# Threshold attention with a leaky-ReLU network: q of the first pair of heads is loaded and split in two pieces

## The chip, the cores and the metric

The kernel runs on one NeuronCore of a Trainium2 chip. A core has a matrix engine (TensorE, PE in the profile, with its weight loads as PEld), VectorE (DVE), ScalarE (ACT), GpSimd (POOL), and SyncE (SP), which in this kernel only issues DMAs. Each engine runs its own instructions in order and waits on semaphores for the others. Matrix results land in PSUM, all other tiles in SBUF. The metric is the device time of one execution in microseconds; the median of several runs is compared.

## The reference

Inputs are q, k, v of shape 8 x 8 x 576 x 64 (batch, heads, sequence, head size) in float32, a number tau = 0.02, and two weight matrices of 512 x 2048 and 2048 x 512.

```
scores = q @ k^T / 8
thresh = max(scores, last axis) - tau
scores = where(scores >= thresh, scores, -1e9)
attn   = exp(scores - max(scores))
attn   = attn / (sum(attn) + 1e-9)
x      = (attn @ v), heads joined to 4608 x 512
h      = x @ w_in
out    = max(0.01 * h, h) @ w_out          (4608 x 512, float32)
```

## The kernel before

The heads are taken two at a time. A *pair* p is two neighbouring heads of one batch; there are 32 pairs, and two pairs make a *chunk* c of nine *steps* t, each step one block of 128 rows of scores (the ninth holds the last 64 rows of both pairs). So the main loop (lines 406 to 480) runs 16 chunks of nine steps and one more chunk that finishes. All is emitted under a manual schedule (line 379): the order of instructions on each engine is the order of the program text.

**Loading.** `load_qk(p, i, tail)` (line 73) issues one DMA on SP's queue: for i = 0 q, for i = 1 k; without `tail` the first 512 rows as four tiles of 128 rows for both heads (256 KB, line 81), with `tail` the last 64 rows (32 KB, line 86). Both fill the tile `nat`, of which three buffers exist. Pair 0 is loaded first, in the order q, k, tail of q, tail of k (line 381). Then the identity matrix and some constants are made, and pairs 1 and 2 are loaded on the same queue (lines 395 to 398). Later pairs are loaded in the loop, two steps' worth ahead (lines 477 to 480); a load into a buffer waits until the pair that was there has been transposed.

**Splitting.** `prep(p, i)` (line 122) turns one operand of a pair round: PE transposes its tiles of 128 rows in float32 into PSUM (line 129; four tiles for q, five for k, since both tails travel with k), ScalarE scales and rounds them to the fp16 tile `hi` (line 138), and VectorE computes the remainder `lo` in fp16 (line 139). The remainder is not emitted at once but put on the list `soon`, which is run at the end of the step (line 467; for pair 0 right behind the two calls, line 401). The PSUM tile of `prep` is A, with a single buffer of two banks; only the k of pair 0 uses a buffer of the scores' tile s instead (line 400). A is also used by the value matmuls and sums of later chunks. A new user of A waits for the last reader of the one before.

**A step.** `s_mm(c, t)` (line 145, matmuls at line 158) computes the scores of one block for both heads as three products, hi hi + lo hi + hi lo, into two s tiles, of which two buffers exist. `s_max` (line 167) runs once per head: VectorE copies the scores out with a sign and takes the row maximum (tile sn, line 181), GpSimd adds tau (nth, line 186), and ScalarE takes the exponential, either plainly (tile e, line 191) or with the threshold in it (tile far, line 197, then W, line 201, with a read of the accumulated row sum). `s_mask` (line 206) applies the threshold on VectorE for the plain ones, one step later, and sends W through a transposing DMA on SP's queue (line 220). In steps 0 and 1 of chunk 0 `prep` of pair 1 stands between the score matmuls and the maxima (lines 429 to 431): q in step 0, k in step 1.

**The rest.** From the second chunk on the values are multiplied (line 279), and from the third on units of the two dense layers (matmuls at lines 301 and 316) are dealt out over the steps by fixed shares. Weights and v come in over GpSimd's queue from step 1 on.

The order of the start is, on PE: transposes of pair 0's q, of its k, scores of step 0, transposes of pair 1's q, scores of step 1, transposes of pair 1's k, scores of step 2.

Of the kernel before, what the change touches and what calls it, by code (L numbers as in the profile page):

```python
# [10 lines left out]
FP16 = mybir.dt.float16  # L11
OP = mybir.AluOpType
AF = mybir.ActivationFunctionType
# [3 lines left out]
def kernel(  # L17
# [10 lines left out]
    nc = tc.nc  # L28
# [8 lines left out]
    QS = 64.0  # L37
# [4 lines left out]
    sb = ctx.enter_context(tc.tile_pool(name="sb", bufs=1))  # L42
# [18 lines left out]
    nat, qk, wTs, xTs = {}, {}, {}, {}  # L61
# [5 lines left out]
    def pair_of_banks(tag="A", bufs=1):  # L67
        return ps.tile([128, 2, 512], FP32, tag=tag, bufs=bufs, name=tag)
# [1 line left out]
    def bank():  # L70
        return ps.tile([128, 512], FP32, tag="u", bufs=2, name="u")

    def load_qk(p, i, tail):

        b, g = divmod(p, NG)
        if p not in nat:
            nat[p] = sb.tile([128, 9, 2, 64], FP32, tag="nat", bufs=3, name="nat")
        t = nat[p]
        h2 = (q, k)[i][b, 2 * g:2 * g + 2, :, :]
        if not tail:  # L80
            nc.sync.dma_start(
                out=t[0:128, 4 * i:4 * i + 4, :, :],
                in_=h2[:, 0:512, :].rearrange("h (p c) d -> p c h d", c=4),
            )
        else:
            nc.sync.dma_start(
                out=t[ds(64 - 64 * i, 64), 8, :, :],
                in_=h2[:, 512:576, :].rearrange("h p d -> p h d"),
            )
# [23 lines left out]
    def take(fs):  # L113
        r = list(fs)
        fs.clear()
        return r

    def run(fs):
        for f in fs:
            f()  # L120

    def prep(p, i, tag="A", bufs=1):


        t = nat[p]
        pt = pair_of_banks(tag, bufs).rearrange("p a b -> p (a b)")
        for c in range(4 + i):

            nc.tensor.matmul(  # L129
                out=pt[0:128, ds(c * 128, 128)],  # L130
                lhsT=t[0:128, 4 * i + c, :, :].rearrange("p h d -> p (h d)"),
                rhs=I32[:, :],
                is_transpose=True, skip_group_check=True,
            )
        N = 512 + 128 * i
        hi = sb.tile([128, N], FP16, tag=f"hi{i}", bufs=3, name=f"hi{i}")
        lo = sb.tile([128, N], FP16, tag=f"lo{i}", bufs=3, name=f"lo{i}")
        nc.scalar.activation(out=hi[:, :], in_=pt[:, 0:N], func=AF.Copy, bias=0.0, scale=QS)  # L138
        soon.append(lambda: nc.vector.scalar_tensor_tensor(  # L139
            out=lo[:, :], in0=pt[:, 0:N], scalar=QS, in1=hi[:, :],  # L140
            op0=OP.mult, op1=OP.subtract,
        ))
        qk.setdefault(p, {})[i] = (hi, lo)

    def s_mm(c, t):

# [75 lines left out]
    inv, rows, rcs = {}, {}, {}  # L222
# [9 lines left out]
    def sums_1(c):  # L232
        d1, rr = inv[c]
        nc.vector.reciprocal(out=rr[:, :], in_=d1[:, :])
        nc.gpsimd.tensor_scalar(out=r2[:, 0, 0:18], in0=rr[:, :], scalar1=1.0 / RS, scalar2=0.0,
                                op0=OP.mult, op1=OP.add)
# [58 lines left out]

    def h_unit(N, xs, g_out, j0, nj):

        t = bank()
        for j in range(nj):
            for gi in range(NG):  # L300
                nc.tensor.matmul(  # L301
                    out=t[:, ts(j, N)], lhsT=w_in16[:, gi, ts(j0 + j, 128)], rhs=xs[gi],
                    start=(gi == 0), stop=(gi == NG - 1), skip_group_check=True,
                )
        nc.scalar.activation(out=g_out, in_=t[:, 0:nj * N].rearrange("p (j n) -> p j n", j=nj),  # L305
                             func=AF.Prelu, bias=0.0, scale=1.0, alpha=0.01)
# [68 lines left out]
    def work(n):  # L375
        for _ in range(min(n, len(units))):
            units.pop(0)[1]()

    with tc.manual_schedule():
        nc.scalar.preload_act_table_set("natural_log_exp_and_others")  # L380
        for i, tail in ((0, 0), (1, 0), (0, 1), (1, 1)):
            load_qk(0, i, tail)
        make_identity(nc, I32)
        nc.vector.tensor_copy(out=I16[:, :], in_=I32[:, :])
        nc.vector.memset(ntau[:, :], -tau_f)
        nc.vector.memset(r2[:, :, :], 0.0)
        nc.vector.tensor_tensor(
            out=sel[:, :, :], in0=I32[:, 0:18].unsqueeze(2).to_broadcast([128, 18, 64]),
            in1=I32[:, 64:82].unsqueeze(2).to_broadcast([128, 18, 64]), op=OP.add,
        )  # L390
        nc.vector.tensor_scalar(out=sel[:, :, :], in0=sel[:, :, :], scalar1=RS, scalar2=None, op0=OP.mult)
        for t in Vs:
            nc.vector.memset(t[64:128, :, 0, 4, :], 0.0)
            nc.vector.memset(t[0:64, :, 1, 0, :], 0.0)
        for p in range(1, 3):
            for i in range(2):
                for tail in range(2):
                    load_qk(p, i, tail)
        prep(0, 0)
        prep(0, 1, "s", 2)  # L400
        run(take(soon))
        share = (23, 27, 23, 13, 23, 13, 23, 23, 23)
        credit = 0.0
        w_at = [1 + i for i in range(32)]
        prev = None
        for c in range(NC + 1):
            last = c == NC
            for t in range(NT):
                step = c * NT + t
                if c > 1 and c % 2 == 0 and t == 6:  # L410

                    if c % 4 == 2 and c > 2:
                        push_tail(c // 2 - 3, 1)
                    push_main(c // 2 - 1)
                    if c % 4 == 0:
                        push_tail(c // 2 - 2, 0)
                    if last:
                        push_tail(c // 2 - 2, 1)
                if not last:
                    s_mm(c, t)  # L420


                nxt = {6: (2 * c + 2, 0), 7: (2 * c + 2, 1), 8: (2 * c + 3, 0), 0: (2 * c + 1, 1)}
                if c == 0:
                    nxt[0], nxt[1] = (1, 0), (1, 1)
                pi = nxt.get(t)
                if pi is not None and pi[0] >= NP:
                    pi = None
                if c == 0 and t < 2:
                    prep(*pi)  # L430
                    pi = None

                if c > 0 and t in (3, 5):
                    values(c - 1, t // 2 - 1)

                ahead = [share[i % NT] for i in range(step, (c // 2 * 2 + (0 if c % 2 == 0 and t < 6 else 2)) * NT + 6)]
                credit = min(credit, 1.0) + (len(units) - credit) * share[t] / sum(ahead)
                n = min(int(credit + 0.01), len(units))
                credit -= n
                if not last:  # L440


                    direct = tau_f <= 16.0 and (
                        t not in (3, 7) if c < 3 else t in (3, 5) or not any(u[0] for u in units[:n]))
                    s_max(c, t, 0, False)
                if c > 0 and t == 1:
                    sums_1(c - 1)
                work(n - n // 2)
                if pi is not None:
                    prep(*pi)  # L450
                if c > 0 and t in (2, 4):
                    sums_4(c - 1, t // 2 - 1)
                if not last:
                    s_max(c, t, 1, direct)
                if c > 0 and t == 1:
                    sums_2(c - 1)
                    work(n // 2 - 1)
                    sums_3(c - 1)
                    work(1 if n > 1 else 0)
                else:  # L460
                    work(n // 2)
                if prev is not None:
                    s_mask(*prev)
                    prev = None
                if not last:
                    prev = (c, t)
                run(take(soon))
                if c > 0 and t == 0:
                    sums_0(c - 1)
                if c == 0 and 0 < t < 6:  # L470
                    load_v(0, t - 1)
                if c % 2 == 0 and c > 0 and t >= 4 and c // 2 < B:
                    load_v(c // 2, t - 4)
                for i in range(32):
                    if w_at[i] == step:
                        load_w(i)
                if t < 4 and 2 * c + 3 < NP:
                    load_qk(2 * c + 3, t // 2, t % 2)
                elif 4 <= t < 8 and 2 * c + 4 < NP:
                    load_qk(2 * c + 4, t // 2 - 2, t % 2)  # L480
        work(len(units))
# [35 lines left out]
```

## Time and profile before

| what | value |
| --- | --- |
| median of 3 runs | 540.57 us (540.03 to 540.68) |
| span of the profiled execution, first to last instruction | 538.3 us |
| mean granted TensorE clock over the span | 0.967 |
| PE busy | 497.8 us, 92% |
| ScalarE busy | 433.8 us, 81% |
| VectorE busy | 421.7 us, 78% |
| GpSimd busy | 188.1 us, 35% |
| first load issued, first transpose, first maximum | 0.75, 4.59, 10.13 us |

Of the profiled execution the span is given; it is 2.3 us shorter than the median of the timed runs, which also hold what lies before the first and after the last instruction. The profile gives, for each group of instructions, the count, the busy time and the mean of one; for each row of the timeline the start, the length, the engine, the line of the kernel, the operation and the tiles written and read, and in brackets how long the engine stood idle before and what released it. Rows that begin with SPq or ACTq are issues of DMAs by that engine's queue. In a table by windows each row has the window, its length, the busy time with the number of instructions in brackets, the granted clock, the DMA engines' share and the rate in GB/s.

### The profile page before, as it was taken

How to read it: one execution, taken by the hardware profiler on the slowest of the kernel's cores; microseconds unless marked ns; L12 is line 12 of the kernel's file. 1: busy time of each engine (PE TensorE's matmuls, PEld its weight loads, DVE VectorE, ACT ScalarE, POOL GpSimd, SP SyncE). 2: the span in 40 equal slices, each digit the busy share in tenths (PEclk: the TensorE clock that was granted, in tenths of full speed). 3: DMA queues.
4: the chain of work that ended last, by engine and by line, in shares of the span. 5: the costliest groups of instructions: out<-in, count | busy, mean ns of one | idle time of the engine just before them, and what ended most of it. 6: DMA issues, size and time to landing. Idle time of an engine off the chain costs nothing.

```text
span 538.3 us, 12333 instructions
## 1 busy us (share of the span) xinstructions
PE 497.8 (92%) x4384; PEld 272.8 (51%) x4384; DVE 421.7 (78%) x1106; ACT 433.8 (81%) x765; POOL 188.1 (35%) x430
## 2 busy tenths in 40 slices
PE   5678679899999999999999999999999999999996
PEld 3345454454545565454545566455545566445444
DVE  4897989988899878987899878987899878982000
ACT  3887879899878989889888989889888989884622
POOL 0754556443433334222432234323432234331000
PEclk9676969999999999999999999999999999999999
DMA  6999999998998699778999799777998699654001
GB/s 151 150 202 161 175 182 214 200 180 173 172 165 136 139 169 196 140 137 153 183 155 143 132 182 185 142 135 159 183 155 136 132 187 135 111 89 106 39 40 58
DMA packets 266814, 80.50 MB, mean 150 GB/s; under 512 B 251905, under 2 KB 264193, under 8 KB 266753
## 3 DMA queue, kind: packets, MB, share of 16 engines
q1 hardware_dynamic: 249136, 70.68, 72.3%
q0 software_dynamic: 17536, 8.92, 14.2%
q8 instruction: 34, 0.56, 0.4%
q14 instruction: 28, 0.22, 0.1%
q10 hardware_dynamic: 80, 0.13, 0.1%
HBM read 36.70 MB, written 9.44 MB: 86 GB/s over the span
## 4 chain that ended last, share of the span: by engine, by line
PE 43%; ACT 25%; DVE 16%; issue 8%; DMA 4%; POOL 3%; SPq 0%; DVEq 0%; ACTq 0%; POOLq 0%
PE u L316 13%; DVE sn L181 11%; PE u L301 10%; PE s L158 10%; PE A L279 8%; ACT e L191 7%; ACT far L197 5%; ACT W L201 5%; DVE W L214 3%; ACT gM L305 3%; ACT hi L138 3%; POOL nth L186 3%; DMA nat<-in_q_dram 2%; DVE lo L139 1%; ACT rc L268 1%
## 5 line engine op out<-in xcount | busy, mean ns | idle before, releaser
L181 DVE TENSOR_SCALAR_CACHE_REDUCE sn<-s 128x576 f32<-128x576 f32 x288 | 206.5, 750 | 49.3 <-PE s L158 49.1
L186 POOL TENSOR_SCALAR nth<-nmx 128x1 f32<-128x1 f32 x288 | 127.4, 442 | 251.7 <-DVE sn L181 229.5
L191 ACT ACTIVATE e<-sn,nmx 128x576 f16<-128x576 f32 x196 | 150.5, 769 | 32.4 <-DVE sn L181 32.2
L214 DVE SCALAR_TENSOR_TENSOR W<-sn,nth,e 128x576 f16<-128x576 f32 x196 | 155.6, 814 | 0.0
L301 PE MATMUL u<-xT,win 128*128 128x512 f16 x512 | 128.9, 380 | 2.5 <-ACT gM L305 2.5
L316 PE MATMUL u<-wout,gM 128*128 128x512 f16 x512 | 126.2, 380 | 0.0
L158 PEld LDWEIGHTS <-hi 64*128 64x128 f16 (+1 forms) x1280 | 65.1, 99 | 70.2 <-issue 54.9
L158 PE MATMUL s<-hi,hi 64*128 64x288 f16 x512 | 86.2, 300 | 10.3 <-DVE sn L181 8.8
L158 PE MATMUL s<-lo,hi 64*128 64x288 f16 (+1 forms) x640 | 92.2, 294 | 0.0
L158 PE MATMUL s<-hi,lo 64*128 64x288 f16 (+1 forms) x640 | 92.1, 294 | 0.0
L301 PEld LDWEIGHTS <-win 128*128 128x128 f16 x768 | 58.7, 98 | 56.5 <-issue 20.1
L305 ACT ACTIVATE gM<-u 128x512 f16<-128x512 f32 x128 | 74.6, 588 | 11.7 <-PE u L301 11.7
L197 ACT ACTIVATE far<-sn,nth 128x576 f32<-128x576 f32 x92 | 71.0, 771 | 13.8 <-POOL nth L186 11.6
L201 ACT ACTIVATE W<-far,ntau 128x576 f16<-128x576 f32 x92 | 71.3, 775 | 3.0
L316 PEld LDWEIGHTS <-gM 128*128 128x128 f16 x512 | 44.7, 98 | 51.3 <-issue 12.3
L139 DVE SCALAR_TENSOR_TENSOR lo<-A,hi 128x512 f16<-128x512 f32 (+1 forms) x63 | 47.6, 756 | 14.2 <-ACT hi L138 13.7
L129 PE MATMUL A<-I,nat 128*128 128x128 f32 x283 | 44.6, 288 | 9.9 <-DVE lo L139 4.7
L279 PE MATMUL A<-wT,V 128*64 128x288 f16 x640 | 47.5, 297 | 1.5 <-ACT rc L268 1.1
L129 PEld LDWEIGHTS A<-I,nat 128*128 128x128 f32 x283 | 35.2, 147 | 25.2 <-DVE lo L139 10.0
L138 ACT ACTIVATE hi<-A 128x512 f16<-128x512 f32 (+1 forms) x63 | 40.0, 636 | 7.6 <-PE A L129 7.6
L279 PEld LDWEIGHTS <-V 128*64 128x64 f16 x640 | 36.6, 113 | 11.9 <-issue 8.4
L158 PEld LDWEIGHTS <-lo 64*128 64x128 f16 (+1 forms) x640 | 32.1, 99 | 12.6 <-issue 8.9
(44 smaller groups left out, 292.1 us busy)
## 6 DMA issues: line engine op xcount, KB each, us to landing
nat<-in_q_dram SPq DMA_DIRECT2D x32, 256.0 KB, 3.8
nat<-in_k_dram SPq DMA_DIRECT2D x32, 256.0 KB, 3.9
out_dram<-osb SPq DMA_DIRECT2D x16, 512.0 KB, 3.0
wT<-W SPq DMA_TRANSPOSE x144, 3.9
V<-in_v_dram POOLq DMA_DIRECT2D x8, 256.0 KB, 6.1
win<-in_moe_w_in_dram POOLq DMA_DIRECT2D x16, 128.0 KB, 5.2
V<-in_v_dram POOLq DMA_DIRECT2D x16, 128.0 KB, 4.7
wout<-in_moe_w_out_dram POOLq DMA_DIRECT2D x16, 128.0 KB, 4.3
```

The source lines that it names most:

```text
L129: nc.tensor.matmul(out=pt[0:128, ds(c * 128, 128)], lhsT=t[0:128, 4 * i + c, :, :].rearrange("p h d -> p (h d)"), rhs=I32[:, :], is_transp ...
L158: nc.tensor.matmul(out=out[h][po, half, 0:288], lhsT=qk[p][i][a][r, cols], rhs=qk[p][1][b][r, ds(half * 288, 288)], start=(ti == 0), stop= ...
L181: nc.vector.tensor_scalar(out=sn[:, h, :].rearrange("p (a b) -> p a b", a=2), in0=s_[:, :, 0:288], scalar1=-BS, scalar2=None, op0=OP.mult, ...
L186: nc.gpsimd.tensor_scalar(out=nth[:, h:h + 1], in0=nmx[:, h:h + 1], scalar1=1.0, scalar2=tau_f, op0=OP.mult, op1=OP.add,)
L191: nc.scalar.activation(out=e[:, h, :], in_=sn[:, h, :], func=AF.Exp, bias=nmx[:, h:h + 1], scale=-1.0,)
L197: nc.scalar.activation(out=far[:, :], in_=sn[:, h, :], func=AF.Prelu, bias=nth[:, h:h + 1], scale=-1.0, alpha=BIG,)
L201: nc.scalar.activation(out=w[:, ds(h * 576, 576)], in_=far[:, :], func=AF.Exp, bias=ntau[:, 0:1], scale=1.0, accum_out=dens[c][:, 2 * t + ...
L214: nc.vector.scalar_tensor_tensor(out=w[:, ds(h * 576, 576)], in0=sn[:, h, :], scalar=nth[:, h:h + 1], in1=e[:, h, :], op0=OP.is_le, op1=OP ...
L279: nc.tensor.matmul(out=t[ds(h * 64, 64), half, 0:288], lhsT=vb[:, g, h, kb, :], rhs=wT[:, 4 * h + kb, ds(e * 576 + half * 288, 288)], star ...
L301: nc.tensor.matmul(out=t[:, ts(j, N)], lhsT=w_in16[:, gi, ts(j0 + j, 128)], rhs=xs[gi], start=(gi == 0), stop=(gi == NG - 1), skip_group_c ...
L305: nc.scalar.activation(out=g_out, in_=t[:, 0:nj * N].rearrange("p (j n) -> p j n", j=nj), func=AF.Prelu, bias=0.0, scale=1.0, alpha=0.01)
L316: nc.tensor.matmul(out=t[:, :], lhsT=g_in(j), rhs=w_out16[:, j, :], start=(j == 0), stop=(j == NJ - 1), skip_group_check=True,)
```

## The change

`load_qk` can load a range of q's four tiles and can issue on another engine's queue. `prep` can split a range of tiles; the range's results go into columns of one shared pair of tiles hi and lo. With these, the start is arranged anew:

- On SP's queue: the first tile of pair 0's q (64 KB), then all of k, and then the other three tiles of q as two DMAs, one for each head (96 KB each).
- On ScalarE's queue, ahead of the load of its function table: the tails of q and k.
- Ahead of the loop only the first tile of q is split, then k with the tails.
- The other three tiles of q are split in step 0 of chunk 0, behind the scores of that step and ahead of the split of pair 1's q. Both splits use A, and both remainders are on `soon`, which runs at the end of the step.

```diff
-    def load_qk(p, i, tail):
+    def load_qk(p, i, tail, eng=nc.sync, c0=0, c1=4):
...
         if not tail:
-            nc.sync.dma_start(
-                out=t[0:128, 4 * i:4 * i + 4, :, :],
-                in_=h2[:, 0:512, :].rearrange("h (p c) d -> p c h d", c=4),
-            )
+            rows = h2[:, 0:512, :].rearrange("h (p c) d -> p c h d", c=4)[:, c0:c1, :, :]
+            for hs in (ds(0, 2),) if c1 - c0 in (1, 4) else (ds(0, 1), ds(1, 1)):
+                eng.dma_start(out=t[0:128, 4 * i + c0:4 * i + c1, hs, :], in_=rows[:, :, hs, :])
         else:
-            nc.sync.dma_start(
+            eng.dma_start(
...
-    def prep(p, i, tag="A", bufs=1):
+    def prep(p, i, tag="A", bufs=1, c0=0, c1=None):
...
+        c1 = c1 or 4 + i
         pt = pair_of_banks(tag, bufs).rearrange("p a b -> p (a b)")
-        for c in range(4 + i):
+        for c in range(c0, c1):
...
-        N = 512 + 128 * i
-        hi = sb.tile([128, N], FP16, tag=f"hi{i}", bufs=3, name=f"hi{i}")
-        lo = sb.tile([128, N], FP16, tag=f"lo{i}", bufs=3, name=f"lo{i}")
-        nc.scalar.activation(out=hi[:, :], in_=pt[:, 0:N], func=AF.Copy, bias=0.0, scale=QS)
+        if i not in qk.setdefault(p, {}):
+            qk[p][i] = [sb.tile([128, 512 + 128 * i], FP16, tag=f"{n}{i}", bufs=3, name=f"{n}{i}")
+                        for n in ("hi", "lo")]
+        w = ds(c0 * 128, (c1 - c0) * 128)
+        hi, lo = (x[:, w] for x in qk[p][i])
+        nc.scalar.activation(out=hi, in_=pt[:, w], func=AF.Copy, bias=0.0, scale=QS)
         soon.append(lambda: nc.vector.scalar_tensor_tensor(
-            out=lo[:, :], in0=pt[:, 0:N], scalar=QS, in1=hi[:, :],
-            op0=OP.mult, op1=OP.subtract,
-        ))
-        qk.setdefault(p, {})[i] = (hi, lo)
+            out=lo, in0=pt[:, w], scalar=QS, in1=hi, op0=OP.mult, op1=OP.subtract))
...
     with tc.manual_schedule():
+        load_qk(0, 0, 0, c1=1)
+        load_qk(0, 1, 0)
+        for i in range(2):
+            load_qk(0, i, 1, nc.scalar)
+        load_qk(0, 0, 0, c0=1)
         nc.scalar.preload_act_table_set("natural_log_exp_and_others")
-        for i, tail in ((0, 0), (1, 0), (0, 1), (1, 1)):
-            load_qk(0, i, tail)
...
-        prep(0, 0)
+        prep(0, 0, c1=1)
         prep(0, 1, "s", 2)
...
                 if c == 0 and t < 2:
+                    if t == 0:
+                        prep(0, 0, c0=1)
                     prep(*pi)
                     pi = None
```

## The prediction

> **What bounds the kernel now.** I read the page's busy shares first, then the chain of work that ended last, in order of time, and from it the timeline of the first 20 us, where the whole change lies.
>
> The page, shares of the span and granted clock in 40 slices of 13.5 us:
>
> ```profile
> PE 497.8 (92%) x4384; PEld 272.8 (51%) x4384; DVE 421.7 (78%) x1106; ACT 433.8 (81%) x765; POOL 188.1 (35%) x430
> ...
> PE   5678679899999999999999999999999999999996
> ...
> PEclk9676969999999999999999999999999999999999
> ```
>
> TensorE (PE) is the bound from slice 9 on; ahead of it no engine is full. What a start-up edit is worth must be read from the chain there (start, length, what):
>
> ```profile
> 0.75 0.78 SPq L81
> ...
> 1.58 4.10 DMA nat<-in_k_dram
> ...
> 5.73 1.34 PE s L129 x5
> ...
> 7.09 0.71 ACT hi L138
> ...
> 7.83 0.84 DVE lo L139
> ...
> 8.71 1.59 PE s L158 x11
> 10.30 1.05 PE A L129 x4
> 11.35 1.68 PE s L158 x11
> ...
> 13.05 0.25 DVE sn L181
> ```
>
> The reader is to see two things. The first scores wait for the landing of k at 5.68, not of q. And from there the chain hands over without a pause: transposes, split, scores of step 0, transposes of pair 1's q (the row at 10.30), scores of step 1. Later pieces of DMA in the chain are few (wT 3.28 us at 314, nat of q 6.83 at 322 and 4.32 at 388, out 2.27 at 333), and each is issued by SP behind the work of its own step, so it shifts along. A microsecond won or lost here moves everything behind it.
>
> The timeline around steps 0 to 2:
>
> ```profile
> 10.23 1.12 PE L129 MATMUL A<-I,nat 128*128 128x128 f32 x4
> ...
> 11.38 0.60 ACT L138 ACTIVATE hi<-A 128x512 f16<-128x512 f32 x1 [3.59 <-PE A L129]
> ...
> 12.01 0.69 DVE L139 SCALAR_TENSOR_TENSOR lo<-A,hi 128x512 f16<-128x512 f32 x1 [0.44 <-ACT hi L138]
> ...
> 15.25 0.82 DVE L139 SCALAR_TENSOR_TENSOR lo<-A,hi 128x640 f16<-128x640 f32 x1
> ...
> 15.99 0.75 DVE L181 TENSOR_SCALAR_CACHE_REDUCE sn<-s 128x576 f32<-128x576 f32 x1
> ```
>
> Today there is one user of PSUM tile A per step: four transposes, the ACT copy to hi, and the DVE remainder lo at the step's end. A has one buffer, so the next user of A waits for that lo.
>
> **The change, part by part.** The sum is made in differences on the profiled execution, whose span is 538.3 us. The runs' median is 540.57, so 2.3 us lie around the span; I add the same 2.3 after the change.
>
> *q's first load cut to a quarter, tails moved.* k is issued at 1.58 as today's second DMA, behind 64 KB in place of 256 KB. The loads of line 81 in the first 30 us show how soon one lands after its issue:
>
> ```profile
> DMA to landing us min/median/max: 3.6/3.8/7.3
> ```
>
> Today k took 4.10, so it was queued behind q for only 0.3 to 0.5 us. With the queue clear, k lands at 1.58 + 3.7 = 5.28: gain 0.4 us. Ends: a quarter-size q may also be issued in 0.62 instead of 0.78 and k then land after the fastest 3.55, gain 0.8; or the 64 KB of tails, sent at the same moment from the other queue, and two queues at once, delay it as far as today's later landings, loss 0.3 (k at 6.0). I take 0.4, by the median row.
>
> A rule of the Trainium skill speaks against the tails' new queue: in "DMA: Bandwidth & Descriptors", section "Issuing engines are not separate DMA queues", DMAs of SP and ScalarE run on the same 16 engines and interleave, and only issue time is saved. In the trace 3.0 to 4.5 us moved 240 to 290 GB/s, so 64 KB are about 0.22 us: by the rule the gain would be 0.2 instead of 0.4.
>
> *SP's queue.* Four issues before pair 1's (q, k, two tails: 0.75 to 3.90), four after (q tile 0, k, two halves of the other three tiles): the loads of pairs 1 and 2 keep their place within some tenths. Pair 1's q, issued at 3.90, lands 3.6 later, at 7.5, and is transposed at 10.2. The three q tiles, issued from about 2.3 and 3.0, land by about 7 and are wanted at 9.8. The load of pair 3's q, which waits at 9.5 for pair 0's last transposes, goes out some 1.2 us later; behind it on SP stands the transposing DMA of 15.3. All hidden.
>
> *ScalarE's queue.* Two issues go ahead of the table load (0.74, 1.28 long). SP's rows for the tails are 0.6 to 0.9 each, so the table is ready at 3.2 to 3.9 and not 2.0. ACT's first copy comes at 5.71 today; of q tile 0 it would be at about 4.2, and the one that counts, hi of k, at 6.7. Cost nothing; without k's wait it would cost 1.5. POOL's queue is not touched.
>
> *First split, q tile 0 alone.* One transpose instead of four; hi and lo of 128 columns, 0.3 each (512 to 640 columns cost 0.10 and 0.13 more, carried down). All before k lands. From k on everything is today's, so step 0's scores end 0.4 earlier: the moment E at which PE starts the transposes behind them moves from 10.23 to 9.83.
>
> *The three other tiles, in step 0.* This is the cost. Their transposes, hi and lo now stand between step 0's scores and pair 1's q, with both tile users on A's one buffer, and lo comes only after both of step 0's maxima on DVE. Counted from E:
> - three transposes: four need 1.15 to the ACT copy, five (13.15 to 14.52) 1.37; three 0.94. hi of 384 columns 0.48, to 1.42. DVE is free at 1.33 (second maximum). lo of 384 columns 0.56, from 1.45 to 2.01.
> - only then do pair 1's transposes start: 2.05, where they start at 0 today. PE idles about 1.1 us in this gap.
> - scores of step 1 stand behind them on PE: 2.05 + 1.05 = 3.10 (today 1.05). Their first maximum needs 1.66 more (today 1.77, with about 0.1 of waiting in it): 4.76, today 2.82.
> - ACT: hi of pair 1 waits for the same transposes, 3.20 to 3.80; then step 0's e, far, W (0.77 each, 0.19 for the sum) to 6.3; then hi of pair 1's k, 6.3 to 7.0 (today 4.29).
> - DVE: two maxima 4.76 to 6.19, mask to 6.93, lo of pair 1's k from 7.03 (today 5.02), first maximum of step 2 at 7.77 (today 5.76).
>
> So step 2 starts 2.0 us later relative to E. PE's own extra work is nil (nine transposes either way), ACT and DVE have one more instruction of some 0.2 each, hidden in these waits. What can differ: if ACT's copies start at once and the wait for lo were only half as long, 1.5; if a full-clock stretch is lost (below), 2.6.
>
> Sum: -0.4 + 2.0 = +1.6; 540.57 + 1.6 = 542.2. The chain shows nothing behind that waits for something other than this work, so nothing takes the delay up.
>
> *The clock.* PE's busy time per 3.41 us cell (granted clock behind it):
>
> ```profile
> 7.87:11.28 3.41, 2.94 (x16) 1.00 0.90 203
> 11.28:14.70 3.42, 3.42 (x21) 1.00 0.35 80
> 14.70:18.11 3.41, 1.70 (x24) 1.00 0.41 63
> 18.11:21.52 3.41, 2.38 (x17) 0.50 1.54 162
> ...
> 59.07:62.48 3.41, 2.10 (x30) 1.00 1.25 192
> 62.48:65.90 3.42, 1.88 (x17) 1.00 1.27 156
> 65.90:69.31 3.41, 1.67 (x12) 0.50 1.26 202
> ```
>
> Before 14.70 nothing is recorded and 1.00 is a filler: score pairs are 0.24 apart there, 0.12 after. Full rate began only behind cells that were busy throughout (14.70, 31.76, 48.83, 76.14), and ended behind cells of 1.9 or less (18.11, 38.59, 65.90). A step at half rate takes 1.48 from a step's last maximum to the next first one, at full rate 0.92: 0.56 us a step. The Trainium skill, "TensorE: Matmul & The Clock Gate", Part 1, has a free-running window of 3413 ns, and half rate after an idle window; the trace agrees on the length and not on the idleness, since half-busy cells sufficed. By the page's rule no cell here would drop the clock, and the change could not touch it.
>
> **Rivals.**
> 1. *k is not earlier.* The tails share the engines with it and it lands at 5.7. For it: tails and k are in flight together; against: 64 KB are 0.22 us at most. Gain 0: 542.6. Chance 0.12.
> 2. *The first full-rate stretch is lost.* With the gap in PE, busy runs from 11.9 to 17.6 fill no cell on today's grid, so step 3's scores run at half rate: 0.56 more, 542.8; one more cell late in a later stretch (3.41 / 2.9 x 0.56 = 0.66), 543.4. Against: where the grid falls in another execution is not shown. Chance 0.13.
> 3. *Small net.* k's gain is 0.8 and the stall 1.5, or the stall is 2.0 and a step more falls at full rate: 541.2 to 541.6, within 0.2%. Chance 0.19.
> 4. *Faster.* The shift moves work into the cells that tripped the clock (1.86 busy up to 38.59, 1.88 up to 65.90; 2.10 held), and full rate lasts from 31.8 on: 20.5 us of half rate, some seven steps of 2.9, times 0.56 = 3.9 won, 538.3. It decides from 2.7 won on. For it: 0.2 us in a cell is enough; against: a 2 us shift of everything moves no work relative to its neighbours, and the grid would have to suit twice. Chance 0.07.
>
> The forecast itself, 542.2, has 0.49; its own range is 541.6 to 542.9.
>
> **How the numbers follow.** The three runs before differ by 0.65 us; 0.2%, or 1.08 us, is about what can be told from no change. Slower (over 541.65): forecast, 1 and 2, 0.74, less 0.02 for the forecast's lower edge, 0.72. Same: rival 3 and that edge, 0.21. Faster: 0.07. The range reaches down through rival 3 and the lower ends of both terms together (0.8 won, 1.5 lost, 0.56 of clock) to 540.6, and up over rival 2 to 543.4; what is left out is rival 4 and the far ends.
>
> **What would show it.** k lands near 5.3 and hi of k starts near 6.7, with tail loads under ACT's queue: the gain. Between step 0's scores and pair 1's transposes, PE shows a wait of about 1.1 us put down to the DVE instruction that makes lo: the stall. The first maximum of step 2 stands near 17.6 instead of 15.99. If PE does not wait there, or step 2's maximum is at 16.5 or earlier, the prediction is wrong in its main term; if that is right and the total is not, the clock's stretches should have moved.

## The result and the profile after

The changed kernel takes 542.17 us in the median, against 540.39 us for the kernel before: 1.0028 times, 95% interval 1.0017 to 1.0039, so 0.9 to 2.1 us slower. Forecast were 542.2 us and a slower kernel. The profiled execution spans 539.9 us against 538.3.

The page of the changed kernel, shares of the span and the clock in 40 slices:

```profile
PE 498.0 (92%) x4384; PEld 272.2 (50%) x4384; DVE 421.6 (78%) x1107; ACT 434.4 (80%) x766; POOL 188.7 (35%) x430
...
PEclk9776969999999999999999999999999999999999
```

Nothing can be read from it: busy times moved by at most 0.6 us, and DVE and ACT have the one more instruction each. The chain in order of time (start, length, what) tells it:

```profile
0.74 0.47 SPq L83
...
1.27 3.87 DMA nat<-in_k_dram
...
9.76 0.85 PE A L129 x3
...
10.63 0.50 ACT hi L140
...
11.15 0.57 DVE lo L141
...
11.77 1.11 PE A L129 x4
12.88 1.60 PE s L157 x12
```

Up to 9.76 it is the old chain, half a microsecond early. Where it then handed over from transposes straight to the scores of step 1, it now goes PE, ACT, DVE and back to PE. The timeline of the changed kernel shows the waits in brackets; that of 1.17 us on lo is where the time is lost:

```profile
9.69 0.90 PE L129 MATMUL A<-I,nat 128*128 128x128 f32 x3
...
11.15 0.56 DVE L141 SCALAR_TENSOR_TENSOR lo<-A,hi 128x384 f16<-128x384 f32 x1
...
11.77 1.11 PE L129 MATMUL A<-I,nat 128*128 128x128 f32 x4 [1.17 <-DVE lo L141]
...
14.47 0.76 DVE L180 TENSOR_SCALAR_CACHE_REDUCE sn<-s 128x576 f32<-128x576 f32 x1 [0.23 <-PE s L157]
...
17.31 0.75 DVE L180 TENSOR_SCALAR_CACHE_REDUCE sn<-s 128x576 f32<-128x576 f32 x1
```

The first maximum of step 0 starts at 9.59 (10.13 before), of step 1 at 14.47 (13.05), of step 2 at 17.31 (15.99), of step 4 at 22.75 (21.26), of step 24 at 84.24 (82.99). From step 24 to the landing of the last output both kernels need the same, 454.3 us. Behind that landing the changed kernel takes another 1.35 us, the one before 0.97. At the end SP waits for one semaphore after another, each wait about 0.06 us. The wait for the last output is the second in this row in the changed kernel and the eighth in the one before, so in the changed kernel more of the others still stand behind it.

### The profile page after: what moved, and what is told of

It reads as the page before. It is cut to its first block, busy times and chain, and to the rows that moved or that the text cites. A ratio compares the mean times of both kernels' runs of the same rounds, so it can differ in the third digit from the quotient of the medians.

```text
span 539.9 us, 12339 instructions
## 1 busy us (share of the span) xinstructions
PE 498.0 (92%) x4384; PEld 272.2 (50%) x4384; DVE 421.6 (78%) x1107; ACT 434.4 (80%) x766; POOL 188.7 (35%) x430
## 4 chain that ended last, share of the span: by engine, by line
PE 46%; ACT 23%; DVE 16%; issue 8%; DMA 3%; POOL 3%; SPq 0%; DVEq 0%; ACTq 0%; POOLq 0%
PE u L315 14%; PE s L157 11%; PE u L300 11%; DVE sn L180 11%; PE A L278 8%; ACT e L190 6%; ACT far L196 5%; ACT W L200 5%; DVE W L213 3%; ACT hi L140 3%; ACT gM L304 3%; POOL nth L185 2%; DVE lo L141 2%; DMA nat<-in_q_dram 1%; PE A L262 1%
```

## The experiments

The theory had two terms: k comes earlier (a gain of about half a microsecond), and a second user of PSUM tile A in step 0 makes pair 1's transposes wait for a whole round trip (a loss of 2 us). The rival explanations were that the new order and queue of the loads cost the time, that the added work does, or that the clock does. The table has each kernel's profiled execution (k's landing, the first maximum of steps 0, 2, 8 and 24) and its timing against the kernel before, all in us.

| kernel | k lands | step 0 | step 2 | step 8 | step 24 | median | ratio to before, interval |
| --- | --- | --- | --- | --- | --- | --- | --- |
| before | 5.68 | 10.13 | 15.99 | 33.06 | 82.99 | 540.3 to 540.7 | 1 |
| changed | 5.14 | 9.59 | 17.31 | 34.56 | 84.24 | 542.17 | 1.0028, 1.0017 to 1.0039 |
| late split alone | 5.62 | 10.07 | 17.79 | 35.43 | 85.82 | 542.46 | 1.0033, 1.0021 to 1.0046 |
| free bank | 5.00 | 9.45 | 15.88 | 33.51 | 84.40 | 540.84 | 1.0016, 1.0001 to 1.0032 |
| two turns of A | 5.25 | 9.70 | 18.64 | 35.68 | 86.66 | 544.10 | 1.0062, 1.0037 to 1.0086 |
| tails on SP | 4.77 | 9.21 | 17.02 | 34.06 | 84.44 | 541.91 | 1.0027, 1.0003 to 1.0051 |
| early split | 5.18 | 9.63 | 15.39 | 33.16 | 82.11 | 540.44 | 1.0003, 0.9989 to 1.0016 |
| k first | 4.54 | 9.70 | 15.46 | 32.50 | 83.74 | 540.39 | 1.0001, 0.9992 to 1.0010 |
| early split, tails on SP | 4.88 | 9.33 | 15.20 | 32.23 | 82.54 | 539.54 | 0.9986, 0.9977 to 0.9996 |
| q tile beside k | 4.38 | 8.83 | 14.61 | 32.09 | 81.42 | 539.48 | 0.9989, 0.9970 to 1.0008 |

From step 24 to the landing of the last output all ten profiled executions need between 454.1 and 454.3 us. The row of waits behind it takes 0.97 and 0.98 us in the two kernels with the four loads of before (before, late split alone), and 1.34 to 1.35 in the eight with the six new ones. So a total with the new loads holds 0.37 us that neither term explains. Which part of the new loads sets the order of these waits, was not tried.

**The late split alone.** The loads as before the change; only the split is in two pieces.

```diff
-        load_qk(0, 0, 0, c1=1)
-        load_qk(0, 1, 0)
-        for i in range(2):
-            load_qk(0, i, 1, nc.scalar)
-        load_qk(0, 0, 0, c0=1)
         nc.scalar.preload_act_table_set("natural_log_exp_and_others")
+        for i, tail in ((0, 0), (1, 0), (0, 1), (1, 1)):
+            load_qk(0, i, tail)
```

> The loads as before the change, and only the late split of q's three other tiles kept. Theory (the loss is the second turn of PSUM tile A in step 0): k lands at 5.7, the first maximum of step 2 starts near 17.9 instead of 15.99, and the total is 2.0 us over the kernel before, 542.4. Rival (the loss comes from the new order and queue of the loads): as the kernel before, 540.4, with step 2 at 16.0.

Its timeline has the same wait:

```profile
12.25 1.11 PE L129 MATMUL A<-I,nat 128*128 128x128 f32 x4 [1.17 <-DVE lo L141]
...
17.79 0.75 DVE L180 TENSOR_SCALAR_CACHE_REDUCE sn<-s 128x576 f32<-128x576 f32 x1
```

k lands at 5.62, step 2 starts at 17.79, and the total is 0.33% over the kernel before. The loss is there without the new loads. That rival is out, and the theory's first number (17.9) and its total (542.4) hold.

**A free bank.** The three tiles go into a bank of tile u, which has no other user before the dense layers begin.

```diff
-        pt = pair_of_banks(tag, bufs).rearrange("p a b -> p (a b)")
+        pt = bank() if tag == "u" else pair_of_banks(tag, bufs).rearrange("p a b -> p (a b)")
...
-                        prep(0, 0, c0=1)
+                        prep(0, 0, "u", 2, c0=1)
```

> The changed kernel, with the three tiles of q transposed into a free bank of tile u instead of A. Theory: pair 1's transposes no longer wait for lo, what is left is three transposes more on PE (0.9) ahead of the scores of step 1; step 2's first maximum near 16.3 instead of 17.31, total 540.8. Rival (the loss is the added work and not the wait on A): no different from the changed kernel, 542.2, step 2 at 17.3.

The chain of that run, in order of time:

```profile
9.62 0.83 PE u L129 x3
10.45 0.85 PE A L129 x4
11.31 1.75 PE s L157 x11
```

Both sets of transposes now stand behind each other on PE, without the trip over ACT and DVE. Step 1 starts at 13.04 instead of 14.47 with the same work, and the median is 540.84, as expected. Counted from the first transpose behind step 0's scores, step 1 comes after 3.49 (4.78 in the changed kernel, 2.82 before). So 1.29 of the 1.96 lost there is the wait on A. The 0.67 that is left is about the 0.70 by which pair 1's transposes start later on PE, behind the three that were moved there. Step 2 came earlier than expected (15.88 against 16.3): k had landed at 5.00, and the five transposes of pair 1's k ran at full rate (the clock was full from 12.95 on in this execution). The agreement of the median is not explained by this. At step 2 this execution is 0.11 ahead of the kernel before; it falls 0.45 behind only at step 3, whose scores ran at half rate, and the waits at the end add their 0.37.

**Two turns.** The three tiles are split in two turns of A, so that step 0 has three users.

```diff
-                        prep(0, 0, c0=1)
+                        prep(0, 0, c0=1, c1=2)
+                        prep(0, 0, c0=2)
```

> The changed kernel, with the three tiles of q split in two turns of tile A (one tile, then two), so that step 0 has three users of A instead of two. Theory (each turn is a round trip of PE, ACT and DVE): pair 1's transposes start 1.05 later, step 2's first maximum near 18.4 instead of 17.31, total 543.2. Rival (a fixed loss from splitting late at all): 542.2, step 2 at 17.5 at most.

Its timeline, with the wait of each turn in brackets:

```profile
11.40 0.69 PE L129 MATMUL A<-I,nat 128*128 128x128 f32 x2 [1.12 <-DVE lo L141]
...
13.02 1.11 PE L129 MATMUL A<-I,nat 128*128 128x128 f32 x4 [0.93 <-DVE lo L141]
```

Each turn of A stops PE for about a microsecond. Pair 1's transposes start at 13.02 instead of 11.77, 1.25 later. Of this 0.11 is k, which landed later in this execution; one more turn costs 1.14 (1.05 expected). The total rises to 1.0062; the 544.10 us are 0.9 over the 543.2 expected, which its interval still holds. The loss grows with the number of turns and is not a fixed price of splitting late.

**Tails on SP.** The changed kernel with the tails back on SP's queue, behind k.

```diff
-            load_qk(0, i, 1, nc.scalar)
+            load_qk(0, i, 1)
```

> The changed kernel, with the two tails back on SP's queue, behind k. If tails on another queue hold k up (they share the DMA engines), k lands 0.2 earlier, near 4.9, and the total is 542.0. If k's own issue and its size set its landing, k lands at 5.1 as in the changed kernel and the total is 542.2.

The chain's piece for k:

```profile
0.75 0.46 SPq L83
...
1.26 3.51 DMA nat<-in_k_dram
```

Issued at the same moment as in the changed kernel, k needs 3.51 instead of 3.87 and lands 0.37 earlier (0.2 expected). In the four profiles with the tails on ScalarE's queue and k behind the q tile on SP's it took 3.7 to 4.0, in the two with all on SP 3.5 and 3.6. So with the tails on a queue of their own, which frees issue time on SP, k takes a third of a microsecond longer. That agrees with the rule of the Trainium skill ("DMA: Bandwidth & Descriptors", "Issuing engines are not separate DMA queues") that DMAs of different issuing engines interleave on the same 16 DMA engines and that only issue time is saved.

How much of it the tails' own data does, is not shown. With the tails gone from SP's queue, the loads of q's other three tiles are issued 1.4 us earlier too (at 2.07 instead of 3.45). From 2.75 us to k's landing the changed kernel moved some 1940 packets for SP's queue, 1024 of them k's, and 145 for ScalarE's; with the tails on SP it was some 1330 in all. So some 900 packets of the loads behind k, q's other tiles first, ran beside it, and fewer of the tails. No run with k in the same place moves the one without the other. The total cannot tell so little: its interval is half a per cent wide.

**Early split.** The loads of the changed kernel, but the three tiles are split ahead of the loop, behind k.

```diff
         prep(0, 1, "s", 2)
         run(take(soon))
+        prep(0, 0, c0=1)
+        run(take(soon))
...
-                    if t == 0:
-                        prep(0, 0, c0=1)
```

> The loads of the changed kernel, but the three tiles of q are split ahead of the loop, behind k. They land by 5.9, and PE, ACT and DVE have gaps there. Theory (both terms as forecast): the 0.54 us of earlier k are kept and the stall is gone; step 2's first maximum at 15.45, total 539.9. Rival (the split delays k's hi or lo, which the first scores wait for): half a microsecond or more later, 540.4 or above. Rival (early gains are taken up later): 540.4 although step 2 is early.

The timeline of PE shows the three extra transposes (the second row) and the first scores' waits for k's hi and lo:

```profile
5.22 1.33 PE L129 MATMUL s<-I,nat 128*128 128x128 f32 x5 [1.87 <-DMA nat<-in_k_dram]
6.35 0.85 PE L129 MATMUL A<-I,nat 128*128 128x128 f32 x3
7.35 0.39 PE L157 MATMUL s<-hi,hi 64*128 64x288 f16 x1 [0.15 <-ACT hi L140]
8.21 0.39 PE L157 MATMUL s<-hi,hi 64*128 64x288 f16 x1 [0.47 <-DVE lo L141]
```

The extra transposes, hi and lo fall into the time in which PE waits for k's hi and lo, and cost the first scores nothing: step 0 at 9.63 as in the changed kernel, step 2 at 15.39 (15.45 expected). But step 3 starts at 18.30, only 0.04 ahead of the kernel before. Why, the table of PE's busy time by clock cells shows (granted clock behind the busy time):

```profile
9.76:13.17 3.41, 3.41 (x20) 1.00 0.62 141
13.17:16.58 3.41, 1.87 (x17) 1.00 0.10 17
16.58:19.99 3.41, 2.18 (x15) 0.50 1.35 161
```

In this execution the cells fell so that the stretch at full clock ended at 16.58, before all but one of step 3's score matmuls, which ran at half rate. The total, 540.44, is the second rival's number, but it can be told neither from before nor from the 539.9 expected, which also leaves out the 0.37 of the waits at the end. Whether the start's half microsecond arrived at the end, this run leaves open.

**k first.** As the early split, with k as SP's first DMA and the q tile as its second.

```diff
-        load_qk(0, 0, 0, c1=1)
         load_qk(0, 1, 0)
-        for i in range(2):
+        load_qk(0, 0, 0, c1=1)
+        for i in (1, 0):
             load_qk(0, i, 1, nc.scalar)
```

> As the early split, but k is the first DMA on SP, then one tile of q, tails of k and q on ScalarE's queue, then the three tiles. Theory (k's landing is its issue plus 3.7): k lands near 4.5 as q did before the change, scores start 0.65 earlier than in the early split; step 2's first maximum at 14.8, total 539.3. Rival (k is held by what shares the engines, not by its own issue): k lands near 5.0, total 539.8.

k did land at 4.54, and it helped nothing against the early split: on PE the q tile's transpose still stood ahead of k's, and the q tile, now second, landed at 4.98. Step 0 started at 9.70 instead of the 9.0 that the expectation implied. The chain shows the change of owner:

```profile
1.57 3.41 DMA nat<-in_q_dram
...
5.12 0.45 PE A L129
5.57 1.08 PE s L129 x5
```

A transfer issued first is worth what the first instruction in the reader's queue makes of it. The total, 540.39, is above both expectations (539.3 and 539.8). Between steps 8 and 24 this execution lost 1.30 us against the kernel before, 0.94 of it in step 12, where the first value matmuls stand:

```profile
45.47 1.35 PE L278 MATMUL A<-wT,V 128*64 128x288 f16 x10
48.34 0.80 PE L278 MATMUL A<-wT,V 128*64 128x288 f16 x10 [1.52 <-DMA wT<-W]
```

The transposed W of step 8 had not landed. It is the only one of these profiles in which PE waits there; whether this order of loads brings it about, was not tried.

**The two lessons together.** The early split with the tails on SP, and the same with the q tile on ScalarE's queue beside k.

```diff
 # early split, tails on SP
-            load_qk(0, i, 1, nc.scalar)
+            load_qk(0, i, 1)
 # q tile beside k: also
-        load_qk(0, 0, 0, c1=1)
+        load_qk(0, 0, 0, nc.scalar, c1=1)
```

> The early split (three tiles of q ahead of the loop, behind k), with the tails on SP's queue behind k. Theory (tails on the other queue held k up by 0.3 to 0.4): k lands at 4.8 instead of 5.18, the first maximum at 9.2 instead of 9.63, that of step 2 at 15.0, total 539.5, a microsecond under the kernel before. Rival (the landing of 4.77 in the run with tails on SP was chance): 5.1 to 5.2 again, first maximum 9.6, total 540.0. If the total is 540.4 although the first maximum is at 9.2, the stretches at half clock between steps 3 and 24 decide and not the start.

> As the last, but the one tile of q goes on ScalarE's queue at the same moment as k on SP's, k thus being SP's first DMA. If k's landing goes by its issue (0.75 instead of 1.27), k lands near 4.5 and the first maximum is at 8.9, total 539.3. If 64 KB sent beside it delay k as the tails did (0.4), k lands at 4.7 to 4.9, first maximum 9.2, total 539.5.

The first gives 539.54, the 539.5 expected; its ratio of 0.9986 (0.9977 to 0.9996) is just clear of no change, and the changed kernel's is on the other side of 1. k's earlier landing came again (4.88; 4.8 expected), and the first maxima of steps 0 and 2 are 0.1 and 0.2 later than expected (9.33 and 15.20). Its chain hands over as before the change, only earlier:

```profile
1.26 3.62 DMA nat<-in_k_dram
...
9.51 1.05 PE A L129 x4
10.55 1.87 PE s L157 x12
```

In the second k lands at 4.38, 3.63 us after its issue and so not held up by the q tile beside it, and step 0 starts at 8.83 (8.9 expected). Its median, 539.48, is no better, with an interval that holds no change too; the half microsecond between the two is below what these timings resolve.

## Why the prediction was right

- *k earlier by 0.4.* It was 0.54 (5.14 against 5.28 forecast). The two halves of the step were each off: the issue of a quarter-size q takes 0.47 instead of 0.78, so k goes out at 1.27 and not at 1.58; and it then takes 3.87 and not 3.7, with the tails and more of q's other tiles in flight beside it. The prediction had both as ends of its range and neither in its sum. Its bound for the tails was 0.22 "at most"; at the 240 to 290 GB/s that it cites, 64 KB are 0.23 to 0.27. The run with the tails on SP has 0.36, which holds the share of the other tiles too.
- *ScalarE's queue, cost nothing.* The table load starts at 2.16 and ends at 3.44, and the first copy follows at 3.45: here the table did end last, since the q tile had landed at 2.68, well ahead of the 3.9 us that the 4.2 of the forecast implied. k's hi, at 6.55, hid it as forecast.
- *The stall, 2.0.* From the moment PE starts the late transposes (9.69; 9.83 forecast): lo ends at 2.02 (2.01 forecast), pair 1's transposes start at 2.08 (2.05), step 1's scores at 3.12 (3.10), its first maximum at 4.78 (4.76). Only the last link was long: pair 1's hi of k came at 6.04 (6.3), because three of ACT's instructions start about 0.1 ahead of the recorded end of the one before (e at 13.41, far at 14.08, the read of W's sum at 15.56), and step 2 at 7.62 (7.77). So the stall was 1.86 at step 2.
- *The sum, +1.6.* At step 2 it was +1.32 (the first maximum at 17.31; 17.6 forecast), at step 4 +1.49, at step 24 +1.25, over the two spans +1.6, and in the medians +1.78. So the two terms together cost less than forecast: the gain was larger and the stall smaller. What brought the spans to the forecast +1.6 was a term that the prediction did not have, the 0.38 by which the waits behind the last output are longer. The agreement of the total to 0.03 us is luck: the forecast counts from 540.57, while the runs of before that the result is compared with have 540.39, and the interval of the ratio is 1.2 us wide. The lower end of the range, from the prediction's own terms (0.8 won, 1.5 lost, 0.56 of clock), is 540.7 and not 540.6.
- *The clock.* The forecast kept the stretches as they were, and in this pair of profiles they are: full rate for one, two and five cells, at 15.82, 32.89 and 49.95, each about 1.1 later than before, and for good from 77.26. These rows of the changed kernel answer to those shown of before:

```profile
12.41:15.82 3.41, 3.41 (x21) 1.00 0.30 68
15.82:19.23 3.41, 1.75 (x21) 1.00 0.30 50
19.23:22.65 3.42, 2.48 (x19) 0.50 1.43 170
```

  The first stretch was not lost, as rival 2 had it, since the long busy run from 11.77 filled a cell; it ended at 19.23 within step 3's scores, which is the step from +1.32 to +1.50. The grid had moved by 1.1 us against the program's start, which the prediction had left open. That it moved by about as much as the work, so that the stretches fell on the same steps, was luck.
- *Shifts arrive in full.* The prediction argued from the chain that nothing takes a delay up. The table bears it out on average: by step 8 the kernels lie between 0.97 ahead and 2.62 behind, and the medians between 0.8 ahead and 3.4 behind, in the same order. For a gain it was too sure: with k first, a transposing DMA ended last at step 12, and with the early split alone the gain does not show in the median.

## What to carry to other kernels

A tile with one buffer has a price per user: the round trip over all engines that touch it, about 1.3 of the 2 us of path here for a split of 384 columns, even though PE does no more work. The rest was the three transposes themselves, which stood ahead of those that the next step needed. Before work is moved later, look whether it falls into a gap of the new place, with a buffer of its own, or behind someone's; the same three transposes cost nothing while PE waited for k's hi and lo. And a transfer made smaller helped the next one by its shorter issue (0.31 of the 0.54 us here) and by what the queue had held it up (0.23); the second is read from the landing time of one on a clear queue, not from the bytes.

## What the runs showed of the hardware beyond that

The cells by which the clock is granted, 3.41 us long, do not start with the program. The first stretch at full rate began at between 12.49 and 18.46 us in the ten profiled executions, and the grids differ by arbitrary fractions of a cell (14.70 and 15.82 in the kernels before and after, 12.95 and 13.17 with the free bank and the early split). Counted over all of them up to step 24, full rate began only behind cells in which PE was busy for 3.0 us or more and ended only behind cells with 2.04 or less, so the two thresholds of the prediction (busy throughout, 1.9) were a little too sharp. Neither holds the other way round. With the early split a cell of 3.41 us, busy throughout, was followed by another at half rate (from 30.23), and with k first full rate held behind a cell of 1.84 (from 46.62).

This moves the time of the stage between step 8 and step 24. With the same instructions in it, it took from 48.95 us (early split) to 51.24 (k first), and nearly all of the spread is in two steps, 12 and 21, where the value matmuls stand in the path: step 12 took 2.77 to 4.58 us and step 21 2.77 to 4.23. The short ones had about half of these matmuls or more at full rate (step 12 with the tails on SP, 2.77, from 47.08 and at full rate from 48.00), the long ones none or few (step 21 there, 4.23, at half rate from 65.07 to 78.72); the longest, 4.58, was the wait for the transposing DMA shown above. After step 24, with the clock full for good, nothing differs by more than 0.2 us up to the landing of the last output. A spread of two microseconds in one execution is larger than the half microseconds that the loads are worth, and it is why a gain seen in step 2 can be missing in one execution's total.
